# Four column pairs of an MLP's first product computed as seven block products instead of eight

## The chip, the cores and the metric

One NeuronCore of a Trainium2 chip runs the whole program in one launch. The metric is device time in microseconds (us) of that launch. PE is the tensor engine, DVE the vector engine, ACT the scalar engine, POOL GpSimd, SP the engine that issues most transfers.

## The reference

The layer has an attention part and an MLP that mixes tokens. S = 2048 tokens, D = 512 channels, F = 1792 hidden units, all in 32-bit floats.

```
h  = x + attention(layernorm(x)) @ wo            # 32 heads, linear attention
hn = layernorm(h)                                # (S, D)
u  = gelu(einsum("sd,sf->fd", hn, w1) + b1)      # (F, D): the first product
y  = einsum("fd,fs->sd", u, w2) + b2             # (S, D): the second product
out = h + y
```

The first product is a sum over the 2048 tokens for each of 1792 x 512 outputs, the second a sum over the 1792 hidden units. Each needs the matrix that the stage before it makes.

## The kernel before, in words

**Tiles.** The tokens are 16 tiles of 128 (`NT`), the hidden units 14 column blocks of 128 (`NF`), taken in 7 pairs (`NP`). PE takes its factors in a type (F32R) that holds less than a 32-bit float, so every factor is split: ACT copies it to that type (the *high* part), DVE or POOL subtracts that from the original (the *low* part), and `mm3` multiplies high by high, high by low and low by high into one accumulator. So each block product is three matmuls, at L65, L66 and L67.

**Stages.** Up to 172 us the keys and values are projected and the key-value sums are built. From 172 to 262 us the attention loop (`for it in range(NT + 4)`) runs over the token tiles: queries, `s_num`, the output projection `s_wo`, `s_h` (h = x + attention), `s_hn` (normalised h) with its split. In `s_hn` ACT writes the normalised tile to a two-buffer scratch `hn`, ACT makes its high part and POOL the low part (L61), and both are kept for all 16 tokens in tiles named `hs`. The order of PE, DVE and ACT is written out by hand in this loop (`ms`, a manual schedule), and closed behind it.

**The first product.** `fill(p)` multiplies token tile t by the two column blocks of pair p: two times three matmuls of 512 columns, with the 128x128 piece of w1 held in PE and the 512 channels of hn streamed past it. A pair is 16 such fills, 96 matmuls. `stream` brings in w1 for two token tiles at a time: one 256 KB transfer, a high copy on ACT (L614), a low subtraction on DVE (L606), each of 512 elements per partition, in rings of four buffers. Pairs 0 and 1 are filled inside the attention loop, `LAG = 5` tiles behind. The rest of pairs 0 and 1 and pairs 2 to 6 come after the loop, from 262 to 379.7 us; there a list scheduler sets the order on each engine and may move a later pair's matmul ahead of one that would wait.

**Between the products.** Behind each pair ACT applies gelu (L730). The second product is already done by seven block products, so its operands are seven 256-channel combinations of the four blocks of u: for pairs 0 and 1 made on POOL with the splits in two large pieces (`near`), for pairs 2 to 6 on DVE with 256-element splits (`far`, tiles `uf`), all of them behind the last pair.

**The second product**, from 379.7 to 518 us, takes w2 in 28 groups: a 512 KB load, three DVE sums (L785 to L787), a 1792-element high copy on ACT (L796), a 1792-element low subtraction on DVE (L805), then matmuls of 512 columns (L834) and 256 columns (L838). Its first three groups are let go by a gate, `issue_after(LO[-18])` and `issue_after(LD[-20])`, the 18th last low part and the 20th last load of w1. Its order is again by hand.

**The seven products.** With four blocks on either side of a two by two block product, the second product forms for each pair seven sums of the weight blocks and seven of the other operand, multiplies them pairwise and combines the seven results. `LAST` and `PROD` list which sum goes with which and into which accumulator.

Of the kernel before, what the change touches and what calls it, by code (L numbers as in the profile page):

```python
# [12 lines left out]
ALU = mybir.AluOpType  # L13
# [12 lines left out]
NG = 8  # L26
NPR = 2 * NG
# [9 lines left out]
def block_kernel(ctx: ExitStack, tc: tile.TileContext, x, xT, wT, phic, wo, w1, b1, w2, b2,  # L37
# [15 lines left out]
    cst.tile([P, 80], F32, name="pad")  # L53
# [15 lines left out]

    aq = ExitStack()  # L70
# [4 lines left out]
    wqh = wqp.tile([P, KD, D], F32R, name="wqh")  # L75
    wql = wqp.tile([P, KD, D], F32R, name="wql")
# [361 lines left out]
    WO = {}  # L438
    for j in range(KD):
        WO[j] = w2p.tile([P, D], F32, name=f"wo{j}")  # L440
        nc.sync.dma_start(WO[j], wo[j * P:(j + 1) * P, :])
# [76 lines left out]
    wst = ExitStack()  # L518
    wf = wst.enter_context(tc.tile_pool(name="wf", bufs=4, reuse_waits="tile"))
    a2 = ExitStack()  # L520
    ak = a2.enter_context(tc.tile_pool(name="ak", bufs=2, reuse_waits="tile"))
    ps_t = a2.enter_context(tc.tile_pool(name="ps_t", bufs=1, space=PSUM, reuse_waits="tile"))
# [52 lines left out]
    def s_h(t):  # L575

        h = HT[t]
        VE[t] = ak.tile([P, 4], F32, name="ve2", bufs=3)
        nc.vector.scalar_tensor_tensor(h, PO.pop(t), 1.0, h, op0=ALU.mult, op1=ALU.add, accum_out=VE[t][:, 2:3])
        nc.sync.dma_start(out[t * P:(t + 1) * P, :], h)  # L580

    def s_moments(t):
# [4 lines left out]
        nc.scalar.activation(VE[t][:, 0:1], VE[t][:, 3:4], AF.Identity, scale=(1.0 + EPS) / D, bias=eps2)  # L587

# [3 lines left out]
    def s_hn(t):  # L592
        nc.scalar.activation(VE[t][:, 1:2], VE[t][:, 1:2], AF.Copy, scale=r2[:, t:t + 1])
        hn = ak.tile([P, D], F32, name="hn")
# [3 lines left out]

    w1v = w1.rearrange("(k p) f -> p k f", p=P)

# [7 lines left out]
    def stream(src, k0, n, c0, w):  # L608

        raw = wf.tile([P, n, w], F32, name="wraw")  # L610
        wh_ = wf.tile([P, n, w], F32R, name="whi")
        wl_ = wf.tile([P, n, w], F32R, name="wlo")
# [34 lines left out]

    for it in range(NT + 4):
        even = it % 2 == 0
        if 0 <= it + 1 < NT:  # L650
            s_pq(it + 1)
# [7 lines left out]
        if it > 1 and even and it <= NT:  # L659
            s_num(it // 2 - 1)  # L660
        den = s_den(it + 2) if it + 2 < NT else []
# [32 lines left out]
        if not logits:  # L694
            flush()
        if 0 <= it - 2 < NT:
            s_h(it - 2)
        flush()
        for p in range(2):
# [3 lines left out]
    ms.close()  # L703
# [3 lines left out]

    up = ctx.enter_context(tc.tile_pool(name="up", bufs=1, side="right", reuse_waits="tile"))
    uo = ctx.enter_context(tc.tile_pool(name="uo", bufs=2, side="right", reuse_waits="tile"))
    ws = ctx.enter_context(tc.tile_pool(name="ws", bufs=2, side="right", reuse_waits="tile"))
# [5 lines left out]
    up.tile([P, 120], F32, name="pad")  # L724
# [7 lines left out]

    def operands_u(p):
        u = U[p]
        tt = ut.tile([P, 3, HD], F32, name="tt")
        e = nc.gpsimd if p < NEAR else nc.vector
        e.tensor_sub(tt[:, 0], u[:, 0], u[:, 1])
        e.tensor_sub(u[:, 0], u[:, 2], u[:, 0])
        e.tensor_sub(tt[:, 1], u[:, 2], tt[:, 0])
        e.tensor_sub(tt[:, 2], u[:, 3], tt[:, 1])  # L740
        if p < NEAR:
            for n0, src in ((0, u), (4, tt)):
                o = near[p][:, n0:n0 + src.shape[1]]
                split(o[:, :, 0], o[:, :, 1], src, nc.vector)
            for m in range(7):
                UB[p, m] = near[p][:, m]
            return
        for m in range(7):
            at = (p - NEAR) * 7 + m
            if at % 2 == 0:  # L750
                far[at // 2] = big.tile([P, 2, 2, HD], F32R, name="uf", tag="big")
            UB[p, m] = far[at // 2][:, at % 2]
            split(UB[p, m][:, 0], UB[p, m][:, 1], u[:, m] if m < 4 else tt[:, m - 4], nc.vector)

    for p in range(NP):
        while FN[p] < NT:
            fill(p, ps_b)
        for c in range(2):
            gelu(2 * p + c, PU[p][c])
        if p < NEAR:  # L760
            operands_u(p)
# [3 lines left out]
    hp = ctx.enter_context(tc.tile_pool(name="hp", bufs=1, reuse_waits="tile"))  # L765

# [211 lines left out]
```

## Time and profile before

| | |
|---|---|
| median of 3 runs | 523.35 us (523.15 to 523.65) |
| the profiled execution | 523.61 us |
| its span in the trace | 521.8 us |
| busy, share of the span | PE 99%, DVE 74%, ACT 54%, POOL 46% |
| granted PE clock | full in every slice of the span |

The span is what lies between the first and the last recorded instruction, 1.8 us less than the device's time. Busy shares are averages over stages with different limits. Recorded durations of neighbouring matmuls overlap: starts lie 0.22 to 0.23 us apart where durations are 0.39 us. So the pace of a row of matmuls is read from start to start, or from a stretch divided by the number of matmuls in it.

### The profile page before, as it was taken

What the parts mean: (1) busy time and instruction counts of PE and PEld (TensorE: products, weight loads), DVE (VectorE), ACT (ScalarE), POOL (GpSimd) and SP (SyncE); (2) the same over time, 40 slices, a digit from 0 to 9 for tenths busy, and PEclk for the clock granted to TensorE, in tenths of its full rate; (3) what the DMA queues carried; (4) which work ended last, traced back from release to release, by engine and by line L of the source; (5) the groups of instructions that cost most, each with busy time, mean ns of one, the idle gap of its engine ahead of it and who ended that gap; (6) DMA issues with size and microseconds to landing.
All of it is one profiled execution on the core that took longest, in us unless ns stands there. A gap on an engine that the chain in (4) does not pass through costs nothing.

```text
span 521.8 us, 8917 instructions
## 1 busy us (share of the span) xinstructions
PE 515.2 (99%) x3379; PEld 435.8 (84%) x3379; DVE 386.0 (74%) x681; ACT 282.0 (54%) x496; POOL 239.6 (46%) x188
## 2 busy tenths in 40 slices
PE   8999999999999999999999999999999999999997
PEld 7888888887877767887788888888889999999997
DVE  6893999986899998773227423725869899988985
ACT  5999853435246876666956423625553424434430
POOL 2479799985999999874425000000002112112220
PEclk9999999999999999999999999999999999999999
DMA  8644211021041324344323354532215686678734
GB/s 299 200 131 121 75 41 38 1 69 36 21 122 49 96 98 125 118 125 137 103 85 118 102 162 155 168 100 82 62 59 109 164 190 147 130 170 180 166 49 81
DMA packets 36298, 58.52 MB, mean 112 GB/s; under 512 B 3744, under 2 KB 19360, under 8 KB 36256
## 3 DMA queue, kind: packets, MB, share of 16 engines
q1 hardware_dynamic: 31936, 51.37, 31.5%
q0 software_dynamic: 4032, 6.42, 9.7%
q8 instruction: 26, 0.43, 0.4%
q10 hardware_dynamic: 288, 0.17, 0.1%
q14 instruction: 16, 0.13, 0.1%
HBM read 46.81 MB, written 11.14 MB: 111 GB/s over the span
## 4 chain that ended last, share of the span: by engine, by line
PE 89%; POOL 7%; DVE 2%; DMA 1%; issue 1%; SPq 0%; ACT 0%; POOLq 0%
PE py L834 16%; PE pu L65 12%; PE pu L66 12%; PE pu L67 11%; PE py L838 10%; PE pv L66 3%; PE pv L67 3%; PE pv L65 3%; PE pk_ps L65 2%; PE pk_ps L67 2%; PE pk_ps L66 2%; POOL ez L447 2%; POOL eq L465 2%; PE po L66 2%; PE po L65 2%; PE po L67 2%
## 5 line engine op out<-in xcount | busy, mean ns | idle before, releaser
L66 PE MATMUL pu<-hs,whi 128*128 128x512 f32 x224 | 87.7, 391 | 1.1 <-POOL hs L61 1.1
L65 PE MATMUL pu<-hs,whi 128*128 128x512 f32 x224 | 87.5, 395 | 0.0
L67 PE MATMUL pu<-hs,wlo 128*128 128x512 f32 x224 | 87.1, 390 | 0.0
L606 DVE TENSOR_TENSOR wlo<-wraw,whi 128x512 fp32r<-128x512 f32 x56 | 43.7, 784 | 53.2 <-ACT whi L614 53.0
L899 POOL DMA_DIRECT2D out<-ot x7 | 6.2, 885 | 151.1 <-DVE ot L895 151.1
L796 ACT ACTIVATE whi<-wraw 128x1792 fp32r<-128x1792 f32 x28 | 47.4, 1701 | 46.0 <-DVE wraw L787 19.8
L805 DVE TENSOR_TENSOR wlo<-wraw,whi 128x1792 fp32r<-128x1792 f32 x28 | 56.5, 2021 | 11.7 <-PE py L838 9.4
L614 ACT ACTIVATE whi<-wraw 128x512 fp32r<-128x512 f32 x56 | 34.9, 628 | 49.6 <-PE pu L66 45.3
L65 PEld LDWEIGHTS pu<-hs,whi 128*128 128x128 f32 x224 | 42.1, 188 | 10.7 <-issue 2.5
L66 PEld LDWEIGHTS pu<-hs,whi 128*128 128x128 f32 x224 | 42.1, 188 | 10.4 <-POOL hs L61 2.1
L834 PE MATMUL py<-uf,whi 128*128 128x512 f32 x175 | 49.8, 395 | 0.0
L67 PEld LDWEIGHTS pu<-hs,wlo 128*128 128x128 f32 x224 | 42.1, 188 | 8.7
L447 POOL TENSOR_TENSOR ez<-eq,zB 128x1024 f32<-128x1024 f32 x16 | 38.3, 2398 | 4.4 <-ACT zB L494 4.4
L838 PE MATMUL py<-uf,whi 128*128 128x256 f32 x210 | 39.1, 283 | 0.0
L200 POOL TENSOR_TENSOR pk<-pk,sk 128x1024 f32<-128x1024 f32 x16 | 31.0, 1940 | 7.6 <-DVE sk L199 5.1
L534 ACT ACTIVATE pht<-tn 128x512 f32<-128x512 f32 x32 | 17.4, 595 | 30.2 <-PE tn L532 30.2
L465 POOL TENSOR_TENSOR eq<-eq,w 128x1024 f32<-128x1024 f32 x16 | 32.2, 2015 | 1.3 <-DVE w L462 1.3
L838 PEld LDWEIGHTS py<-uf,whi 128*128 128x128 f32 x210 | 32.8, 192 | 0.0
L834 PEld LDWEIGHTS py<-uf,wlo 128*128 128x128 f32 x175 | 28.5, 189 | 5.0
L61 POOL TENSOR_TENSOR hs<-hn,hs 128x512 fp32r<-128x512 f32 x16 | 21.6, 1349 | 23.7 <-ACT hs L60 23.7
L204 POOL TENSOR_TENSOR zacc<-zacc,pk 128x1024 f32<-128x1024 f32 x13 | 31.3, 2405 | 0.6
L834 PEld LDWEIGHTS py<-uf,whi 128*128 128x128 f32 x175 | 29.1, 190 | 2.7
(179 smaller groups left out, 1331.9 us busy)
## 6 DMA issues: line engine op xcount, KB each, us to landing
wraw<-in_w SPq DMA_DIRECT2D x56, 256.0 KB, 2.8
wraw<-in_w SPq DMA_DIRECT2D x28, 512.0 KB, 4.4
xraw<-in_xT SPq DMA_DIRECT2D x16, 256.0 KB, 3.0
xh<-in_x SPq DMA_DIRECT2D x16, 256.0 KB, 2.7
h<-in_x SPq DMA_DIRECT2D x16, 256.0 KB, 2.7
out<-h SPq DMA_DIRECT2D x16, 256.0 KB, 2.6
out<-ot POOLq DMA_DIRECT2D x14, 256.0 KB, 4.7
wraw<-in_wT SPq DMA_DIRECT2D x12, 256.0 KB, 5.2
```

What stands on the lines that cost most here:

```text
L65: nc.tensor.matmul(o, ah, bh, start=first, stop=False)
L66: nc.tensor.matmul(o, ah, bl, start=False, stop=False)
L67: nc.tensor.matmul(o, al, bh, start=False, stop=last)
L204: nc.gpsimd.tensor_add(zacc, zacc, PK[t])
L447: nc.gpsimd.tensor_mul(EZ[t], EQ[t], zB)
L465: nc.gpsimd.tensor_mul(heads(EQ[t]), heads(EQ[t]), W[t].rearrange("p g c h -> p (g c h)").unsqueeze(2).to_broadcast([P, 2 * H, DH]))
L606: LO.append(nc.vector.tensor_sub(wl_, raw, wh_).ins)
L614: nc.scalar.activation(wh_, raw, AF.Copy)
L796: nc.scalar.activation(WH[g], RAW[g], AF.Copy)
L805: nc.vector.tensor_sub(wl_, RAW[g], WH[g])
L834: nc.tensor.matmul(o, w, u, start=p == 0 and not low, stop=p == NP - 1, skip_group_check=True)
L838: nc.tensor.matmul(bank[bk][:, half], AW[sp, p][x][:, a], UB[p, b][:, y], start=p == 0 and half == 0 and i == 0, stop=p == NP - 1 and i == ...
```

## The change

Pairs 2, 3, 4 and 5 (`SEVEN`) of the first product are computed as seven block products over pairs of token tiles. A step is one pair of columns by one pair of tokens: seven products of a 128x128 sum of w1 blocks with a 256-channel sum of normalised h blocks, three matmuls of 256 columns each, 21 in all. Eight steps make a pair and 32 the stage. Pairs 0, 1 and 6 stay as they were; pair 6 comes behind the new stage.

- **Sums of w1.** For every step DVE makes the sums in place in the raw tile (`seven_sum`: 256, 128 and 128 elements), ACT copies the 896 elements to the high part, and DVE subtracts for the low part (`seven_lo`). The rings hold 4 raw, 3 high and 3 low tiles.
- **Sums of h.** They are made once: `s_hn` now writes into a kept tile `hb`, `t_sums` forms four sums of a token pair in place, `t_hi` and `t_lo` split them (1024 elements each) into kept tiles `ht`. For token pairs 0 to 3 wholly, and for the sums of 4, this happens inside the attention loop at places given by the table `T_AT`, the rest behind it.
- **Results.** Behind each pair `seven_out` combines four accumulators on DVE (seven operations of 256) and ACT, then gelu. `near_ops` makes the operands of pairs 0 and 1 inside the new stage.
- **Order.** The manual schedule `ms` stays open to the end of the new stage. The rests of pairs 0 and 1 (`fill(0)`, `fill(1)`, `fill(1)`) stand directly behind the loop.
- **Memory.** Tiles named `hold` and `keep` are shared in turn by the query and output weights, `ht` and the w2 groups. The first w2 loads are now gated by `LO[-9]` and `LD[-8]`. The output rows of tokens 14 and 15 are sent from ACT's queue instead of SP's. The output weights `wo` are loaded into `wor`, which is free earlier, so their loads stand earlier in SP's queue.
- **Splits of `far`.** Those of pairs 2 to 6 take two sums at a time (512 elements) where they lie side by side.

```diff
@@ the attention loop @@
+    T_AT = {(13, 2): "a0 b0", (14, 1): "c0 d0", (14, 2): "a2 b2", (14, 3): "h0", (15, 0): "h1", (15, 2): "c2 d2 l0", (15, 3): "h2",
+            (16, 1): "l1", (16, 2): "l2", (17, 2): "a4 b4 c4 d4", (17, 3): "h3", (18, 2): "l3"}
...
     flush()
-    ms.close()
+    fill(0)
+    fill(1)
+    fill(1)
+    assert FN[:2] == [NT, NT]
@@ sums of normalised h @@
-        hn = ak.tile([P, D], F32, name="hn")
...
+        hn = HB[i][:, 2 * k:2 * k + 2].rearrange("p h d -> p (h d)")
...
+    def t_sums(i, half):
+
+        b = [BOTH[i // 2][:, :, m] if i < 6 else HB[i][:, m] for m in range(4)]
+        o, x, y = (((1, 0, 1), (0, 2, 0)), ((2, 2, 1), (3, 3, 2)))[half // 2][half % 2]
+        nc.vector.tensor_sub(b[o], b[x], b[y])
...
+        nc.scalar.activation(HT7[i][0], HB[i], AF.Copy)
+
+    def t_lo(i):
+        nc.vector.tensor_sub(HT7[i][1], HB[i], HT7[i][0])
@@ the new stage @@
+    AT, DEEP = {}, {"raw": 4, "hi": 3, "lo": 3}
...
+        if k == 0:
+            nc.vector.tensor_add(raw[:, 0:2], raw[:, 1].unsqueeze(1).to_broadcast([P, 2, P]), raw[:, 2:4])
+            return
+        nc.vector.tensor_add(raw[:, 4 + k], raw[:, 1 if k == 1 else 4], raw[:, 2 if k == 1 else 5])
+        if k == 2:
+            ready["hi"] += 1
+            wh_ = ring_tile("hi")
+            nc.scalar.activation(wh_, raw, AF.Copy)
...
+        for a, b, bk, half in LAST:
+            for k, (x, y) in enumerate(((0, 0), (0, 1), (1, 0))):
+                nc.tensor.matmul(ACC[p][bk][:, half], WS[p, i][x][:, a], hb[b][y],
+                                 start=i == 0 and half == 0 and k == 0, stop=i == NT // 2 - 1 and k == 2,
+                                 skip_group_check=True)
...
+    for n, (p, i) in enumerate(RUN):
+        seven_step(p, i)
+        many = 2
+        seven_lo()
+        seven_load()
+        sum_with(*todo[:many])
+        todo = todo[many:]
+        if heavy:
+            op = heavy.pop(0)
+            op and op()
+        if i == 1 and p > SEVEN[0]:
+            todo += seven_out(p - 1)
+        if i == 2 and 0 < p - SEVEN[0] <= NEAR:
+            late = near_ops(p - SEVEN[0] - 1)
...
+        if n == len(RUN) - 4:
+            fill_load(NP - 1)
+        if n >= len(RUN) - 2:
+            fill_load(NP - 1)
+            flush()
+    ms.close()
+    for op in todo + seven_out(SEVEN[-1]):
+        op()
@@ the second product @@
-    with tc.issue_after(LO[-18]), tc.issue_after(LD[-20]):
+    with tc.issue_after(LO[-9]), tc.issue_after(LD[-8]):
```

Three places show how the instructions move. The first is PE's order where the last token tile of normalised h comes in, at the end of the attention loop. In the kernel before, `hs_3168` is token tile 15, `pu_2131` an accumulator of pair 0, and `pu_3249` one of pair 2.

```order
L65 MATMUL pu_3249<-hs_2170,whi_3244 128x512
L66 MATMUL pu_3249<-hs_2170,whi_3244 128x512
L67 MATMUL pu_3249<-hs_2170,wlo_3245 128x512
L65 MATMUL pu_3250<-hs_2170,whi_3244 128x512
L66 MATMUL pu_3250<-hs_2170,whi_3244 128x512
L67 MATMUL pu_3250<-hs_2170,wlo_3245 128x512
L65 MATMUL pu_3249<-hs_2249,whi_3264 128x512
L65 MATMUL pu_2131<-hs_3168,whi_3080 128x512
L65 MATMUL pu_2132<-hs_3168,whi_3080 128x512
L65 MATMUL pu_2231<-hs_3168,whi_3125 128x512
L65 MATMUL pu_2232<-hs_3168,whi_3125 128x512
L66 MATMUL pu_3249<-hs_2249,whi_3264 128x512
```

In the kernel after, at the same place, `hs_3165` is tile 14, `hs_3190` tile 15, and `pu_2141` and `pu_2142` are the accumulators of pair 0.

```order
L66 MATMUL pu_2141<-hs_3165,whi_3097 128x512
L67 MATMUL pu_2141<-hs_3165,whi_3097 128x512
L68 MATMUL pu_2141<-hs_3165,wlo_3098 128x512
L66 MATMUL pu_2142<-hs_3165,whi_3097 128x512
L67 MATMUL pu_2142<-hs_3165,whi_3097 128x512
L68 MATMUL pu_2142<-hs_3165,wlo_3098 128x512
L66 MATMUL pu_2141<-hs_3190,whi_3097 128x512
L67 MATMUL pu_2141<-hs_3190,whi_3097 128x512
L68 MATMUL pu_2141<-hs_3190,wlo_3098 128x512
L66 MATMUL pu_2142<-hs_3190,whi_3097 128x512
L67 MATMUL pu_2142<-hs_3190,whi_3097 128x512
L68 MATMUL pu_2142<-hs_3190,wlo_3098 128x512
```

Pair 2's matmuls no longer stand between tiles 14 and 15; tile 15 of pair 0 now follows tile 14 of pair 0 at once, ahead of tile 14 of pair 1. The new stage (L903) follows tile 15 of pair 1.

The second place is DVE's order behind the last `s_h` of the loop (L579 before). Before, low parts of w1 (`wlo`) follow it one after the other.

```order
L606 TENSOR_TENSOR wlo_3081<-wraw_3079,whi_3080 128x512
L579 SCALAR_TENSOR_TENSOR h_2958,ve2_3121<-po_3096,h_2958 128x512
L606 TENSOR_TENSOR wlo_3126<-wraw_3124,whi_3125 128x512
L606 TENSOR_TENSOR wlo_3245<-wraw_3243,whi_3244 128x512
L606 TENSOR_TENSOR wlo_3265<-wraw_3263,whi_3264 128x512
L606 TENSOR_TENSOR wlo_3283<-wraw_3281,whi_3282 128x512
L606 TENSOR_TENSOR wlo_3301<-wraw_3299,whi_3300 128x512
L606 TENSOR_TENSOR wlo_3319<-wraw_3317,whi_3318 128x512
```

After, shortly behind the same `s_h`, there stand sums of w1 (L868, L870), sums of normalised h (L629), the low part of the first step (L891) and low parts of the sums of h (L641).

```order
L870 TENSOR_TENSOR wraw_3247<-wraw_3247 128x128
L629 TENSOR_TENSOR hb_3069<-hb_3069 128x256
L870 TENSOR_TENSOR wraw_3247<-wraw_3247 128x128
L868 TENSOR_TENSOR wraw_3249<-wraw_3249 128x256
L629 TENSOR_TENSOR hb_3069<-hb_3069 128x256
L870 TENSOR_TENSOR wraw_3249<-wraw_3249 128x128
L629 TENSOR_TENSOR hb_3069<-hb_3069 128x256
L870 TENSOR_TENSOR wraw_3249<-wraw_3249 128x128
L891 TENSOR_TENSOR wlo_3272<-wraw_3247,whi_3260 128x896
L641 TENSOR_TENSOR ht_3262<-hb_2762,ht_3262 128x1024
L868 TENSOR_TENSOR wraw_3251<-wraw_3251 128x256
L641 TENSOR_TENSOR ht_1737<-hb_2762,ht_1736 128x1024
```

One stream of 512-element subtractions has become a stream of 128- to 1024-element operations of four kinds.

The third place is DVE's order between the products. Before, the last `far` splits (`uf`) are followed by low parts and sums of w2 (L805, L785 to L787).

```order
L61 TENSOR_TENSOR uf_4098<-tt_4078,uf_4098 128x256
L805 TENSOR_TENSOR wlo_4175<-wraw2_4121,whi_4130 128x1792
L785 TENSOR_TENSOR wraw3_4179<-wraw3_4179 128x512
L786 TENSOR_TENSOR wraw3_4179<-wraw3_4179 128x256
L787 TENSOR_TENSOR wraw3_4179<-wraw3_4179 128x256
L805 TENSOR_TENSOR wlo_4216<-wraw0_4132,whi_4177 128x1792
L785 TENSOR_TENSOR wraw1_4220<-wraw1_4220 128x512
L786 TENSOR_TENSOR wraw1_4220<-wraw1_4220 128x256
```

After, L62 are the `far` splits, L811 to L814 their sums, L1024 the low parts of w2 and L844 to L846 its sums; `wlo1_4665` belongs to the fourth w2 group, and `u_4457` is the u of pair 6.

```order
L813 TENSOR_TENSOR tt_4530<-u_4457,tt_4530 128x256
L846 TENSOR_TENSOR wraw_4581<-wraw_4581 128x256
L1024 TENSOR_TENSOR wlo_4624<-wraw_4570,whi_4579 128x1792
L844 TENSOR_TENSOR wraw3_4628<-wraw3_4628 128x512
L814 TENSOR_TENSOR tt_4530<-u_4457,tt_4530 128x256
L62 TENSOR_TENSOR uf_4535<-u_4457,uf_4535 128x2x256
L62 TENSOR_TENSOR uf_4538<-u_4457,uf_4538 128x2x256
L62 TENSOR_TENSOR uf_4541<-tt_4530,uf_4541 128x2x256
L845 TENSOR_TENSOR wraw3_4628<-wraw3_4628 128x256
L62 TENSOR_TENSOR uf_4544<-tt_4530,uf_4544 128x256
L846 TENSOR_TENSOR wraw3_4628<-wraw3_4628 128x256
L1024 TENSOR_TENSOR wlo1_4665<-wraw_4581,whi_4626 128x1792
```

The sums and low parts of w2 now stand among the operands of the last pair instead of behind them, and the splits take up to 512 elements at a time.

230 lines of the change are left out of this document (187 added, 43 removed).

## The prediction

> **What bounds the kernel now.** I read the page first, then windows by stage, the engines' timelines around the hand-overs, and the groups of DVE and ACT.
>
> ```profile
> PE 515.2 (99%) x3379; PEld 435.8 (84%) x3379; DVE 386.0 (74%) x681; ACT 282.0 (54%) x496; POOL 239.6 (46%) x188
> PE 89%; POOL 7%; DVE 2%; DMA 1%; issue 1%; SPq 0%; ACT 0%; POOLq 0%
> ```
>
> PE is busy 515.2 of 521.8 us, and the chain that ended last runs through it for 89%. So time changes by the work taken from PE less the waits that appear on it. The windows give the stages (columns: window, length, busy and count of PE, PEld, DVE, ACT, POOL, then PE clock, DMA share, GB/s):
>
> ```profile
> 172.00:262.00 90.00, 88.85 (x598) 70.20 (x597) 61.51 (x130) 67.91 (x147) 68.49 (x51) 1.00 0.36 112
> 262.00:380.00 118.00, 118.00 (x522) 97.79 (x521) 58.58 (x105) 54.05 (x96) 9.66 (x11) 1.00 0.39 116
> 358.00:379.80 21.80, 21.80 (x98) 18.07 (x97) 15.97 (x41) 12.61 (x32) 0.00 (x0) 1.00 0.25 72
> 400.00:519.00 119.00, 118.62 (x803) 109.44 (x801) 103.83 (x156) 45.85 (x47) 23.46 (x27) 1.00 0.68 143
> ```
>
> The first product, 262 to 380 us, is bound by PE alone: no idle time in 118 us, while DVE is busy for half of it and ACT for 46%. The attention loop, 172 to 262 us, leaves PE 1.15 us of idle time and DVE 28.5. From 400 us DVE is already busy 87%, so a backlog carried over the hand-over at 380 us would be given back slowly.
>
> **PE's saving.** In the 118 us above are 522 matmuls of 512 columns: 0.226 us each (0.227 from start to start). The 256-column pace is read in the last token pair of the second product:
>
> ```profile
> 502.26 0.40 PE L838 MATMUL py<-un,whi 128*128 128x256 f32 x2
> ...
> 518.10 0.40 PE L838 MATMUL py<-uf,whi 128*128 128x256 f32 x2
> ```
>
> Between these starts lie 44 triples in 15.84 us, so 0.360 a triple and 0.120 a matmul, a little more than half of 0.227. Removed are 4 pairs x 96 = 384 matmuls: 384 x 0.227 = 87.2 us. Added are 32 steps x 21 = 672: 672 x 0.120 = 80.6 us. That is 6.5 us less, and a step lasts 2.52 us, a pair 20.2. The multiplications saved are an eighth of the pairs' columns, 10.9 of 87.2 us; the narrow form gives 4.4 of them back.
>
> [...]
>
> **DVE in the new stage.** Durations and pace, from the second product, where each operation follows another:
>
> ```profile
> 470.61 2.02 DVE L805 TENSOR_TENSOR wlo<-wraw,whi 128x1792 fp32r<-128x1792 f32 x1
> 472.54 0.68 DVE L785 TENSOR_TENSOR wraw<-wraw 128x512 f32<-128x512 f32 x1
> 473.26 0.42 DVE L786 TENSOR_TENSOR wraw<-wraw 128x256 f32<-128x256 f32 x1
> 473.72 0.42 DVE L787 TENSOR_TENSOR wraw<-wraw 128x256 f32<-128x256 f32 x1
> 474.06 2.02 DVE L805 TENSOR_TENSOR wlo<-wraw,whi 128x1792 fp32r<-128x1792 f32 x1
> ```
>
> Start to start, 1792 elements take 1.93 us, 256 before an independent operation 0.34, before a dependent one 0.46, 512 before a dependent one 0.72 (0.60 without). That is N/0.96 ns plus some 0.07 us, and 0.11 more for a dependence. So 896 elements are 1.0, 1024 are 1.13, 128 are 0.20 to 0.31. A step needs one low part and three sums: 1.0 + 0.46 + 0.31 + 0.2 = 2.0 of its 2.52 us; a pair 15.8 of 20.2. A pair also carries `seven_out` of the one before (7 x 0.34 = 2.4 at most) and, twice, near low parts (1024 and 768 elements, 2.0), so at most 20.2 of 20.2: tight. PE's cover is the ring: a low part waits only for its tile to be let go by the matmuls three steps back, so it can be ready about 3 us ahead of its use (two steps of 2.52 less its own 1.0 and the sums between). So DVE costs nothing at a steady pace; were the cover gone, each step over 2.52 us would cost its excess. If each operation cost its full duration, a step would take 1.05 + 0.42 + 2 x 0.30 = 2.07 and the 32 steps 66.2 us; with three `seven_out` of 7 x 0.42 (8.8), the near low parts (2 x 1.49 + 2 x 1.2 = 5.4) and the sums and low parts of the last two token pairs (6.4) DVE would need 86.8 us for the stage's 80.6: a rival, below. ACT copies 1792 elements in 1.70 us and 1024 in 1.07, so 896 in about 0.9: it stays over half free.
>
> ```profile
> L796 ACT ACTIVATE whi<-wraw 128x1792 fp32r<-128x1792 f32 x28 | 47.4, 1701 | 46.0 <-DVE wraw L787 19.8
> L60 ACT ACTIVATE un<-u 128x1024 fp32r<-128x1024 f32 x2 | 2.1, 1066 | 0.0
> L61 DVE TENSOR_TENSOR un<-u,un 128x1024 fp32r<-128x1024 f32 x2 | 3.0, 1490 | 0.5 <-ACT un L60 0.5
> ```
>
> POOL collides with DVE:
>
> ```profile
> 256.99 0.69 DVE L606 TENSOR_TENSOR wlo<-wraw,whi 128x512 fp32r<-128x512 f32 x1
> 262.43 1.09 DVE L606 TENSOR_TENSOR wlo<-wraw,whi 128x512 fp32r<-128x512 f32 x1
> 261.68 1.30 POOL L61 TENSOR_TENSOR hs<-hn,hs 128x512 fp32r<-128x512 f32 x1 [1.92 <-ACT hs L60]
> 275.94 0.73 POOL L739 TENSOR_TENSOR tt<-u,tt 128x256 f32<-128x256 f32 x1
> 276.75 1.07 POOL L740 TENSOR_TENSOR tt<-u,tt 128x256 f32<-128x256 f32 x1
> ```
>
> The same subtraction takes 1.09 instead of 0.69 us beside a POOL operation that ends at 262.98. [...] `near_ops` puts eight such POOL subtractions (0.73 to 1.07 us) into two pairs: up to 3 us more DVE time in each, out of a lead of 3 us. I take nothing for it, up to 2 us at the bad end.
>
> **In the loop.** Sums and low parts of h go into DVE's idle time before `s_h`:
>
> ```profile
> 256.37 0.69 DVE L579 SCALAR_TENSOR_TENSOR h<-po,h 128x512 f32<-128x512 f32 x1 [2.02 <-POOL r L590]
> 261.81 0.69 DVE L579 SCALAR_TENSOR_TENSOR h<-po,h 128x512 f32<-128x512 f32 x1 [4.14 <-issue]
> ```
>
> Two or four 512-element operations (1.2 to 2.7 us) and low parts (1.13) fit gaps of 2.0 and 4.1 us. The tight place is `h2` (ACT, 1.07 us), which stands before the last attention `oh`:
>
> ```profile
> 251.37 1.06 ACT L557 ACTIVATE oh<-tn 128x512 fp32r<-128x512 f32 x2
> 252.47 1.29 DVE L562 TENSOR_TENSOR ol<-tn,oh 128x512 fp32r<-128x512 f32 x2 [2.08 <-ACT oh L557]
> 253.85 0.39 PE L67 MATMUL po<-woh,ol 128*128 128x512 f32 x1
> ```
>
> The first of the two `ol` ends at about 253.1, PE wants it at 253.85: 0.75 us of cover for 1.07, so 0 to 0.5 us is paid; I take 0.3. The moved `wo` loads stand earlier on SP's queue, ahead of an input tile of the first stage; DMA is the releaser on 1% of the chain, so I take 0, up to 0.5. The output rows sent from ACT instead of SP cost ACT an issue each, and SP's loads behind them no longer wait for `s_h`; ACT is idle before 271 us anyway.
>
> **The start of the stage.** Before, pair 2's matmuls stood between token tiles 14 and 15. Now tile 15 comes at once. The first matmul behind the attention's last is at 261.56; 24 matmuls stand ahead of tile 15, so PE wants it at 261.56 + 24 x 0.227 = 267.0:
>
> ```profile
> 261.56 0.39 PE L65 MATMUL pu<-hs,whi 128*128 128x512 f32 x1
> 266.34 0.62 ACT L60 ACTIVATE hs<-hn 128x512 fp32r<-128x512 f32 x1
> 267.04 1.29 POOL L61 TENSOR_TENSOR hs<-hn,hs 128x512 fp32r<-128x512 f32 x1 [2.48 <-ACT hs L60]
> 271.70 1.28 ACT L730 ACT_TABLE_LOAD   x1
> 274.42 1.26 ACT L730 ACTIVATE u<-pu,b1s 128x512 f32<-128x512 f32 x2
> ```
>
> Its high part is ready at 266.96, its low part at 268.33, one matmul after 267.23: a wait of 0.6 to 1.2 us, taken as 0.9. At about 271.7 the stage starts. Its first high parts share ACT with other work. From 266.96 ACT has three high parts of 896 (0.9) and three of 1024 (1.0) in turn, the table load (1.28), four gelus (4 x 0.58 start to start) and then the fourth high part: 266.96 + 5.7 + 1.28 + 2.3 + 0.9 = 277.1, some 278.2 with the gaps between. DVE's low part follows 1.1 later, at 279.3. PE's fourth step begins at 271.7 + 3 x 2.52 = 279.3 and wants it two matmuls on. It comes 0 to 1 us late, the latter if a POOL subtraction of `near_ops` stands in DVE's way; I take 0.5.
>
> **The hand-over.** After the stage's end E, PE has 21.8 us of pair 6 and then the second product. Pair 6 needs low parts of 512, and its second shares a ring tile with its first, so it waits for the matmuls of the first to end: by the paces 0.4 us, and 0.1 at the third; 0.5 in all, between 0 and 1. DVE's order from the last `seven_out` to the low part of the fourth w2 group (`wlo1_4665`) holds 39 operations of 256, 20 of 512 and 4 of 1792: 39 x 0.34 + 20 x 0.60 + 4 x 1.93 = 33.0 us, with dependences about 34.5. Before, DVE had only 15.97 us to do in the 21.80 at that place. Part of the list behind the second product's gate now stands among pair 6's own low parts in DVE's queue, so a w2 load that lands late would hold up pair 6. Counting PE's order from E at 0.227 and 0.120, PE wants this low part at about E + 33.7, and with the waits above at 34.2. The wait is 0 to 2 us (2 if DVE has to wait for ACT on the way); I take 1.0, since no list of this length runs without a gap. The second group's low part is ready at about E + 24, wanted at 26.9. Wider `far` splits (512 in 0.60 for twice 0.34) save DVE time alone.
>
> **The sum.** -6.5 + 0.3 (loop) + 0.9 + 0.5 (start) + 0.5 (pair 6) + 1.0 (hand-over) = -3.3 us. The profiled execution took 523.61 us, 0.26 above the median of 523.35. It becomes 520.3, the median 520.0. A measurement of this kernel can tell about 0.2%, 1.05 us, from no change.
>
> **The rivals.**
>
> *All covers hold (0.14).* Ring leads make up the waits: 523.35 - 6.5 = 516.9. For it: DVE and ACT are half idle there now; against it: tile 15's wait, which nothing covers.
>
> *DVE paces the stage (0.12), the slower side.* Its place is the rings of `wg`. It decides from the point at which a step's DVE work, averaged over a pair, is over 2.52 us. Full durations give 86.8 us against 80.6: the saving is gone, and with the terms at start and hand-over the time is 523.35 - 6.5 + 6.2 + 2.9 = about 526; 525 with a lead kept. For it: those 20.2 us in the two pairs with near operations, and near low parts whose mean was 1.49 beside POOL. Against it: operations in a row start closer than their durations, and two pairs have slack of 2 us.
>
> *The backlog at the hand-over is larger (0.14).* DVE is 87% busy after 400 us, so anything late there is paid by PE. If ACT and DVE wait for each other in the new interleaving of w2 sums, operands and splits, each 1792-element low part comes 1 to 2 us later than its matmuls: three groups, 3 to 6 us more than I took: 523 to 526. For it: my 33.0 us lets DVE wait for nothing. Against it: 20 us of pair 6 in which late work can still be caught up.
>
> *The weight loads set the spacing (0.03).* If a matmul of 256 columns cannot start before its own weight load has run its length, the narrow form saves nothing. In the last window above loads are busy 109.44 us for 801: 0.137 each. 672 x 0.137 = 92.1 us against 87.2, and with the waits 523.35 + 4.9 + 3.2 = 531. Against it: the 44 triples at 0.120 had a load for every matmul too. [...]
>
> **How the numbers follow.** The forecast has 0.57. All waits at their lower ends (0, 0.6, 0, 0.5, 0) give 518.0, at their upper ends (0.5, 1.2, 1, 0.5, 2, and 2 of collisions) 524.0; as they will not all fall together its own range is 518.3 to 522.2. Below it lies 0.14 at about 517. Above lie 0.29, of which I take in those up to 525. Range 516.6 to 525.0. Faster by over 0.2% (under 522.3): 0.57 + 0.14 + 0.01 = 0.72. Within 0.2% (522.3 to 524.4): the better half of the hand-over rival and a little of the DVE rival, 0.10. Slower: 0.18.
>
> **What would show it.** Right: from the last attention matmul on, PE idles in a few places of under 1.5 us (behind tile 14, once in the first four steps, in pair 6 and in the first three w2 groups); 256-column matmuls in the stage start 0.12 us apart, and a pair takes 20.2 us. Wrong: PE waits every step for `wlo` L891 with DVE near 100% (DVE paces); PE waits over 3 us for L1024 or `uf` after pair 6 (backlog); steps over 2.6 us without waits (weight loads).

## The result, and the profile after

| | before | after |
|---|---|---|
| median of 9 runs | 523.15 us (522.74 to 523.65) | 525.48 us (523.85 to 527.03) |
| ratio | 1 | 1.0048 (95%: 1.0036 to 1.0059) |
| the profiled execution, and its span | 523.61, 521.8 | 527.01, 525.2 |

The kernel became 2.3 us slower where 3.3 us less were forecast. The profiled execution is one of four in which PE's mean granted clock was 0.997 (525.8 to 527.0 us); the five with 1.0 took 523.9 to 525.5.

First the busy line of the page after, then windows of the changed kernel over the stretch that the change touches (columns as before the change).

```profile
PE 515.2 (98%) x3667; PEld 445.2 (85%) x3667; DVE 457.8 (87%) x820; ACT 299.3 (57%) x495; POOL 247.6 (47%) x188
```

```profile
262.00:269.00 7.00, 7.00 (x32) 5.66 (x31) 6.86 (x11) 5.71 (x13) 4.42 (x4) 1.00 0.20 74
269.00:278.00 9.00, 7.45 (x27) 5.45 (x26) 8.26 (x18) 7.01 (x10) 1.29 (x1) 0.81 0.21 61
278.00:300.00 22.00, 22.00 (x187) 22.00 (x186) 20.62 (x39) 12.17 (x14) 5.76 (x4) 1.00 0.35 98
300.00:340.00 40.00, 39.70 (x332) 39.50 (x332) 38.17 (x79) 21.32 (x26) 4.67 (x4) 1.00 0.37 103
340.00:380.00 40.00, 39.67 (x253) 35.99 (x253) 37.93 (x82) 24.32 (x38) 0.00 (x0) 1.00 0.43 134
262.00:400.00 138.00, 134.86 (x936) 125.37 (x935) 130.98 (x259) 80.23 (x114) 16.35 (x14) 0.99 0.36 109
```

The same last window of the kernel before:

```profile
262.00:400.00 138.00, 138.00 (x651) 116.00 (x650) 75.01 (x135) 63.63 (x111) 10.70 (x12) 1.00 0.37 108
```

PE's total busy time is the same 515.2 us although 6.5 us of matmuls were taken away. DVE went from 75 to 131 of these 138 us: what was a stage with half of DVE free has become one in which DVE is busy 95%. In the second window the granted clock is 0.81.

The timeline of PE in the changed kernel, from the last attention matmul to the end of the slow stretch (before, the same last matmul stood at 261.33):

```profile
263.95 0.39 PE L68 MATMUL po<-woh,ol 128*128 128x512 f32 x1
...
268.63 0.40 PE L67 MATMUL pu<-hs,whi 128*128 128x512 f32 x1
...
269.57 0.40 PE L68 MATMUL pu<-hs,wlo 128*128 128x512 f32 x1
270.64 0.50 PE L66 MATMUL pu<-hs,whi 128*128 128x512 f32 x1 [0.68 <-ACT hs L61]
272.01 0.50 PE L67 MATMUL pu<-hs,whi 128*128 128x512 f32 x1 [0.87 <-POOL hs L62]
...
272.83 0.63 PE L67 MATMUL pu<-hs,whi 128*128 128x512 f32 x1
273.26 0.63 PE L68 MATMUL pu<-hs,wlo 128*128 128x512 f32 x1
...
275.82 0.58 PE L68 MATMUL pu<-hs,wlo 128*128 128x512 f32 x1
276.23 0.40 PE L66 MATMUL pu<-hs,whi 128*128 128x512 f32 x1
```

Three things are to be seen. The attention ends 2.6 us late, before any matmul of the new stage. From 268.63 to 269.57 four matmuls take 0.235 us each, not 0.227. Tile 15's high and low parts are waited for (2.1 us lost from start to start), and behind that PE runs at half speed from 272.83 to 276.23, eight matmuls 0.427 apart at a granted clock of 0.50.

By stage, span against span (521.84 and 525.23 us):

| place | forecast | measured | read from |
|---|---|---|---|
| matmuls of the four pairs | -6.5 | -6.5 | an undisturbed pair takes 20.1 us (297.70 to 317.78) |
| up to the last attention matmul | +0.3 | +2.6 | 263.95 against 261.33 |
| from there through the first seven-product pair | +1.4 | +3.9 | 33.75 us; PE needs 0.23 + 42 x 0.227 + 20.16 = 29.9 |
| the other three pairs | 0 | +0.4 | 297.70 to 359.48, 61.8 less 0.93 of pair 6 (below), for 60.5 |
| pair 6 and the rest | +1.5 | +2.9 | 165.75 from 359.48 on and those 0.93; 163.76 before |
| sum | -3.3 | +3.3 | spans differ by 3.4 |

Four matmuls of pair 6 stand inside the last step of the stage, ahead of its low part, so their 0.93 us are counted with pair 6:

```profile
356.28 0.40 PE L66 MATMUL pu<-hs,whi 128*128 128x512 f32 x1
...
356.98 0.40 PE L67 MATMUL pu<-hs,whi 128*128 128x512 f32 x1
357.21 0.28 PE L903 MATMUL pu<-hs,wlo 128*128 128x256 f32 x1
```

Of the 3.9 us, 2.1 are tile 15's two waits, 1.6 the eight matmuls at half speed (0.2 us too long each) and 0.2 the slower fills.

### The profile page after: what moved, and what is told of

It reads as the page before. It is cut to its first block, busy times and chain, and to the rows that moved or that the text cites. A ratio compares the mean times of both kernels' runs of the same rounds, so it can differ in the third digit from the quotient of the medians.

```text
span 525.2 us, 9658 instructions
## 1 busy us (share of the span) xinstructions
PE 515.2 (98%) x3667; PEld 445.2 (85%) x3667; DVE 457.8 (87%) x820; ACT 299.3 (57%) x495; POOL 247.6 (47%) x188
## 5 line engine op out<-in xcount | busy, mean ns | idle before, releaser
L1024 DVE TENSOR_TENSOR wlo<-wraw,whi 128x1792 fp32r<-128x1792 f32 x28 | 56.5, 2020 | 6.1 <-PE py L1056 5.3
L874 ACT ACTIVATE whi<-wraw 128x896 fp32r<-128x896 f32 x32 | 30.5, 952 | 38.6 <-DVE wraw L870 26.0
L903 PE MATMUL pu<-ht,whi 128*128 128x256 f32 x256 | 47.2, 282 | 0.0
L67 PE MATMUL pu<-hs,whi 128*128 128x512 f32 x96 | 38.9, 405 | 2.0 <-POOL hs L62 2.0
L66 PE MATMUL pu<-hs,whi 128*128 128x512 f32 x96 | 39.6, 413 | 0.7 <-ACT hs L61 0.7
L903 PEld LDWEIGHTS pu<-ht,whi 128*128 128x128 f32 x256 | 39.7, 191 | 0.0
L68 PE MATMUL pu<-hs,wlo 128*128 128x512 f32 x96 | 37.7, 401 | 0.3 <-DVE wlo L659 0.3
L903 PE MATMUL pu<-ht,wlo 128*128 128x256 f32 x128 | 36.1, 282 | 0.0
L891 DVE TENSOR_TENSOR wlo<-wraw,whi 128x896 fp32r<-128x896 f32 x32 | 34.9, 1092 | 1.3 <-ACT whi L874 1.3
L903 PE MATMUL pu<-hs,whi 128*128 128x256 f32 x192 | 35.9, 283 | 0.0
L62 POOL TENSOR_TENSOR hs<-hb,hs 128x512 fp32r<-128x512 f32 x16 | 22.2, 1385 | 22.8 <-ACT hs L61 20.8
L1056 PEld LDWEIGHTS py<-uf,whi 128*128 128x128 f32 x210 | 32.7, 192 | 0.0
```

What stands on the lines that cost most here:

```text
L66: nc.tensor.matmul(o, ah, bh, start=first, stop=False)
L67: nc.tensor.matmul(o, ah, bl, start=False, stop=False)
L68: nc.tensor.matmul(o, al, bh, start=False, stop=last)
L891: nc.vector.tensor_sub(wl_, raw, wh_)
L903: nc.tensor.matmul(ACC[p][bk][:, half], WS[p, i][x][:, a], hb[b][y], start=i == 0 and half == 0 and k == 0, stop=i == NT // 2 - 1 and k == ...
L1024: nc.vector.tensor_sub(wl_, RAW[g], WH[g])
```

## The experiments

Each was timed beside the kernel before on the same chip. Distances between operands are worked out from the addresses of the tiles in the built programs of these runs, and every pace is read from their traces; the traces do not hold addresses, so what the runs show is how the pace moves when an edit shifts one side or both.

**Where tiles begin.** The first 2.6 us lie where no matmul was added. One line that the excerpt of the diff left out shortens a pad:

```diff
-    cst.tile([P, 80], F32, name="pad")
+    cst.tile([P, 64], F32, name="pad")
```

Every tile of the left side (xs, hs, oh and others) begins 64 bytes lower, and the right side's wqh 32 bytes off. The first experiment is this edit alone, made in the kernel before.

> The kernel before with its first pad tile 64 bytes shorter, so that every tile of the left side of on-chip memory (xs, hs, wvh, the w1 rings, oh, ol) begins 64 bytes lower, as in the changed kernel; nothing else. Theory 1, where an operand begins sets PE's pace, each operand for itself: 512-column matmuls in the first 262 us at about 230 ns instead of 227 and the last attention matmul 2 to 3 us later; the fills of 262 to 380 us at 230 too, so some 1.5 to 2 us more there; 526 to 528 us. Theory 2, only the distance between the two operands counts: projections with weights of the right side (wkh, wqh) slower, fills (hs and whi both moved) unchanged at 227; about 524.5. Theory 3, the layout is not it, the slow pace is a state of that execution: 227 everywhere and 523.2.

523.31 against 522.91 us, 1.0007 (0.9997 to 1.0016). The time hides two opposite moves. The last attention matmul of this kernel:

```profile
262.80 0.39 PE L67 MATMUL po<-woh,ol 128*128 128x512 f32 x1
```

That is 1.5 us later than the 261.33 before, projections running at 230 ns; the second product, 136.4 us from its first to its last matmul instead of 138.5, gives 2.1 back. The fills behind the loop, whose operands moved together, keep 227 ns, all but the first ten, which stand behind slower matmuls and start 231.7 ns apart in the mean. The short rows of fills inside the loop (231 ns) and the first ten of most rows of `wvh` projections, whose operands moved together too, show the same. Theory 1 fails on the fills, theory 3 on the projections; 2 stands, but about ten matmuls behind a slow row were slow too (231.7 ns).

```diff
+    cst.tile([P, 64], F32, name="pad")      # left side
+    wqp.tile([P, 520], F32, name="pad")     # right side, 504 before
```

> The kernel before with left and right side tiles of its first two stages both 64 bytes lower, so that all distances between the operands of a matmul stay as they were while each begins 64 bytes off. Theory 1 (each operand for itself): slower than with the left side alone, 527 to 529 us, projections at 230 ns or more. Theory 2 (distance): 523.2 and 227 ns. Theory 3 (a state of the execution): 523.2.

521.36 us, 0.9966 (0.9953 to 0.9979), faster than any theory said. Projections and fills are back at 227 ns, so in these runs the pace went with the distance, as theory 2 has it. The gain is the second product, where weights had not moved and streamed tiles had: 231.3 ns instead of 232.6 at 512 columns, 116.0 instead of 119.1 at 256.

```diff
-    ones ... r2 = cst.tile(...)
+    ones ... r2 = top.tile(...)             # a pool at the upper end
...                                          # its pad and that of cst
-    wqp.tile([P, 504], F32, name="pad")
+    wqp.tile([P, 512], F32, name="pad")
-        junk = ak.tile([P, D], F32, name="hj", bufs=1)
+        junk = ak.tile([P, D + 104], F32, name="hj", bufs=1)[:, :D]
```

> The changed kernel with the same instructions in the same order, but its constants moved to the upper end of memory and three pads changed, so that all tiles that PE reads begin at multiples of 512 bytes again. Theories 1 and 2: 512-column matmuls before 262 us at 227 ns, the last attention matmul at about 261.5 us instead of 263.95, the whole 2 to 3 us faster, 522.5 to 523.5; the wait for token tile 15 and the slow clock behind it stay. Theory 3: 525.5 and the last attention matmul at 264 as often as before.

523.35 us, 1.0007 (0.9994 to 1.002): 2.1 us below the changed kernel, as theories 1 and 2 said. This is the realigned kernel of what follows. The last attention matmul:

```profile
260.80 0.39 PE L70 MATMUL po<-woh,ol 128*128 128x512 f32 x1
```

The stretch from here through the first pair is still 33.4 us (to 294.16). So the layout accounts for the first term of the error, and not for the second.

**The start of the stage.** In the changed kernel, tile 14 of pair 1 is put ahead and h3, l3 later.

```diff
-    fill(0)
     fill(1)
+    fill(0)
     fill(1)
-(17, 3): "h3", (18, 2): "l3"}
+(18, 2): "h3", (19, 2): "l3"}
```

> The changed kernel with two moves: tile 14 of pair 1 stands ahead of tile 15 of pair 0 on PE, and the high and low parts of the fourth sum of h (h3, l3) come one turn of the loop later, so that they no longer stand on ACT ahead of the normalised h of tile 14. Theory: the two waits behind tile 14 (1.02 and 1.14 us of lost time in the profile) shrink to under 0.7 in sum and the granted clock stays 1.0 behind them, so that 1.4 us of waits and, in the executions that had it, 1.7 us of half-speed matmuls go: 523 to 523.8 instead of 525.5. Rival: the wait is set by the chain through ACT and POOL further ahead (tile 15's own attention), so PE still waits over 1.5 us and the clock falls in some executions: 525.

527.06 us, 1.0077 (1.0062 to 1.0092). Neither theory's time holds. The wait for tile 15 is gone (0.3 us left) and the clock stays 1.0, but PE now waits for three low parts and a high part of w1 in the first five steps, the longest here:

```profile
279.18 0.39 PE L903 MATMUL pu<-hs,wlo 128*128 128x256 f32 x1 [1.42 <-DVE wlo L891]
```

The stretch grew to 35.0 us. Tile 15's wait had been hiding a backlog on DVE, to which this edit adds l3. The next two test that on the realigned kernel.

```diff
     def t_four(i):
-        return [lambda k=k: t_sums(i, k) for k in range(4)]
+        return [None] * 4
     def t_lo(i):
+        if i > 3:
+            nc.gpsimd.memset(HT7[i][1].bitcast(F32), 0.0)
+            return
```

> The realigned changed kernel without eight sums of normalised h (token pairs 6 and 7) and four of their low parts (pairs 4 to 7, filled with zeros on POOL instead), some 8 us less DVE work around the start of the new stage; the output differs by that. Theory A, DVE paces the start: in the realigned kernel PE needs 29.9 us for the matmuls from the end of the attention to the end of the first seven-product pair and takes 33.4, with DVE busy throughout; without the 8 us the stretch falls to 30 to 31 us and the time by 2.5 to 3.5, to about 520.5. Theory B, token tile 15's chain through ACT and POOL sets the start and DVE is only busy beside it: the stretch stays over 32.5 us, 522.5 to 523.4.

The lighter kernel: 522.26 us, 0.9992 (0.9974 to 1.0011); the stretch 32.3 us (260.41 to 292.75), between the two. The wait for DVE that the realigned kernel had in the fifth step (0.83 us from start to start, ending at 284.15) is gone. Tile 15's two waits (0.98 and 0.86 us idle) are not, and they are the 2.4 us by which the stretch still exceeds PE's 29.9. So of the 3.5 us that the realigned kernel loses there, DVE's work is 1.0 and tile 15's chain 2.4. The clock blurs the median: the five executions with a mean clock of 1.0 have 521.55, the five with 0.995 to 0.997 have 523.8 (realigned: 522.7 in four, 523.7 in six).

```diff
-SEVEN = (2, 3, 4, 5)
+SEVEN = (3, 4, 5)
+    for k in range(NT // 2):
+        ...
+        fill(2, ps_b)
+        fill(2, ps_b)
+        ...                       # three of the operations on h
```

> The realigned changed kernel with three pairs of seven products (3, 4, 5) and pair 2 plain, placed ahead of them; the sums of h, their high and low parts and the first sums of w1 are spread beside its 21.8 us of matmuls. Theory A (DVE paces the start): the 3.5 us lost there go but for tile 15's own wait of about 1, one pair's saving of 1.6 us is given up, so about 522.5, and each seven-product pair takes 20.2 us. Theory B (tile 15's chain): the loss at the start stays and 1.6 us are given up, 525.

526.01 us, 1.0063 (1.004 to 1.0086), above both theories. At the start theory A holds but for tile 15's wait: the first seven-product pair begins at 294.6, 2.2 us after PE's own 292.4, nearly all of it tile 15's waits, and takes 20.1. But the loss comes back at the hand-over. A window there and PE's longest wait:

```profile
380.00:396.00 16.00, 13.36 (x81) 11.52 (x80) 15.93 (x29) 8.39 (x12) 0.00 (x0) 1.00 0.42 132
```

```profile
394.18 0.50 PE L1064 MATMUL py<-uf,whi 128*128 128x512 f32 x1 [2.40 <-DVE uf L64]
```

DVE is busy 15.93 of 16 us: the work taken from the start is not gone. Next, which chain makes tile 15 late:

```diff
-(17, 2): "a4 b4 c4 d4", (17, 3): "h3", (18, 2): "l3"}
+(19, 2): "a4 b4 c4 d4 h3 l3"}
```

> The realigned changed kernel with the four sums of token pair 4 and h3, l3 moved behind the last normalised h in the loop, the order of the fills as in the change. Theory: these stood on ACT ahead of tile 14's normalised h and beside POOL's small power operations, and so delayed tile 15; its two waits shrink from 2.3 us to 1.0 to 1.5, near the 0.6 to 1.2 of the prediction, but the moved DVE work then delays the first steps by as much, so 523 to 524.5 in all. Rival: tile 15's chain is late for another reason, waits of 2 us or more and the rest unchanged.

526.9 us, 1.0077 (1.0055 to 1.0099). The waits for tile 15 fell less than expected, from 1.86 us of idle time in the realigned kernel (2.4 lost from start to start) to 1.40 (1.9):

```profile
267.12 0.50 PE L68 MATMUL pu<-hs,whi 128*128 128x512 f32 x1 [0.56 <-ACT hs L63]
268.47 0.50 PE L69 MATMUL pu<-hs,whi 128*128 128x512 f32 x1 [0.84 <-POOL hs L64]
```

From tile 15's `s_h` on DVE to the end of its power on POOL (`r`, which scales the normalised h) it is 2.7 us before the change, 4.3 in the realigned kernel and still 4.0 here. The four sums now run beside POOL's low part of tile 14 and that power:

```profile
262.44 3.83 DVE L631 TENSOR_TENSOR hb<-hb 128x512 f32<-128x512 f32 x4
```

```profile
262.55 1.72 POOL L64 TENSOR_TENSOR hs<-hb,hs 128x512 fp32r<-128x512 f32 x1 [1.94 <-ACT hs L63]
264.23 1.00 POOL L607 TENSOR_TENSOR r<-ve,mhalf 128x1 f32<-128x1 f32 x1
```

The moved work delayed the first steps by more than expected; the stretch is 36.9 us. Last, both limits at once, with the edits of the kernel with the other order and of the lighter one together:

> The realigned changed kernel with both moves at the start: the lighter DVE work (sums of token pairs 6 and 7 and low parts of 4 to 7 left out, zeros instead; the output differs by that), and tile 14 of pair 1 ahead of tile 15 with h3 and l3 one turn later. Theory: the start has two limits, DVE's work and tile 15's chain, and each run so far took away one and ran into the other; with both gone the stretch from the last attention matmul to the end of the first seven-product pair falls from 33.4 to 30 to 30.7 us, and the time to 519.5 to 520.5. Rival: a third wait (ACT's chain of high parts) takes their place: over 31.5 us, 521.5 or more.

521.81 us, 0.9976 (0.9965 to 0.9988), and the stretch is 32.0 us: the rival is right, there is a third limit. Tile 15 is waited for 0.37 us, the fourth step 1.02. PE, and ACT ahead of it:

```profile
280.59 0.39 PE L908 MATMUL pu<-hs,wlo 128*128 128x256 f32 x1 [1.02 <-DVE wlo L896]
```

```profile
274.45 1.28 ACT L792 ACT_TABLE_LOAD   x1
275.75 2.42 ACT L792 ACTIVATE u<-pu,b1s 128x512 f32<-128x512 f32 x4
278.05 1.80 ACT L879 ACTIVATE whi<-wraw 128x896 fp32r<-128x896 f32 x2
```

DVE was idle 2.97 us ahead of that low part, for the high part at 278.05 behind the table load and the gelus. It is the chain that the prediction named for the fourth step.

**Can POOL help DVE?** In the realigned kernel every other low part of w1 goes to POOL:

```diff
-        nc.vector.tensor_sub(wl_, raw, wh_)
+        (nc.gpsimd if ready["lo"] > 4 and ready["lo"] % 2 else nc.vector).tensor_sub(wl_, raw, wh_)
```

> The realigned changed kernel with every other low part of the new stage's w1 blocks on POOL instead of DVE, 14 of 32. DVE gives up 14 x 1.0 us. If two engines can subtract side by side, DVE's waits in the stage go and the time falls 1 to 2 us. If a DVE operation waits while a POOL operation reads memory (as the long low parts beside POOL suggest), a POOL subtraction of about 2.2 us holds DVE up for longer than the 1.0 us it saves, and the stage gets slower: 525 to 529. I expect the latter.

533.75 us, 1.0206 (1.019 to 1.0222), slower still than expected. DVE and POOL at one such place:

```profile
309.35 1.88 DVE L872 TENSOR_TENSOR wraw<-wraw 128x128 f32<-128x128 f32 x1
```

```profile
308.96 2.12 POOL L893 TENSOR_TENSOR wlo<-wraw,whi 128x896 fp32r<-128x896 f32 x1 [3.29 <-ACT whi L876]
```

A sum of 128 elements that takes 0.28 us elsewhere lasts 1.88 and ends 0.15 us after POOL's subtraction at 311.08. At the next such place two of them take 2.51 us from 316.47, where two in a row take 0.60 elsewhere, and end 0.14 us after POOL's subtraction (2.13 us from 316.71). In this kernel idle POOL time was no room for DVE's work of this kind.

**The 64 bytes used on purpose.** Rings of both products 64 bytes further, in the realigned kernel:

```diff
+    wst.enter_context(tc.tile_pool(name="gap", bufs=1, reuse_waits="tile")).tile([P, 16], F32, name="pad")
...
-        WH[g] = keep([P, 7, GRP * P], F32R, "whi", g % 3)
+        WH[g] = off(keep([P, OFF + 7 * GRP * P], F32R, "whi", g % 3))
```

> The realigned changed kernel with the weight rings of the new stage and of the second product 64 bytes further (the identity and the mask moved into another pool to make room), so that weight and streamed operand of the narrow matmuls begin 64 bytes apart modulo 512. With both shifted alike or not at all the narrow form took 119 to 120 ns, with streamed tiles 64 bytes below the weights 113 to 115 in the second product of the kernel with both sides lowered. Theory: distance sets the pace, so the new stage's 672 matmuls take 113.5 to 115 (3.5 to 4.4 us less) and the second product's 2 to 3 us less; DVE then paces two of the pairs, so 517 to 519. Rival: the narrow pace there came from something else, and it stays at 523.4.

521.75 us, 0.9961 (0.9944 to 0.9979), short of the theory's 517 to 519. Two triples of this kernel's stage, then two of the changed kernel's:

```profile
306.02 0.39 PE L906 MATMUL pu<-ht,whi 128*128 128x256 f32 x2
306.25 0.28 PE L906 MATMUL pu<-ht,wlo 128*128 128x256 f32 x1
306.36 0.39 PE L906 MATMUL pu<-ht,whi 128*128 128x256 f32 x2
```

```profile
309.86 0.40 PE L903 MATMUL pu<-hs,whi 128*128 128x256 f32 x2
310.10 0.28 PE L903 MATMUL pu<-hs,wlo 128*128 128x256 f32 x1
310.22 0.40 PE L903 MATMUL pu<-hs,whi 128*128 128x256 f32 x2
```

0.34 us a triple instead of 0.36. Over the whole stage the mean is 115.4 ns instead of 120, so 3.1 us of matmuls went in the stage alone, but 1.6 us of the median in all: where PE is quicker it waits more for DVE (0.77, 0.53 and 0.59 us idle at 284, 318 and 332 in the stage, 0.67 and 0.22 in the realigned kernel, and 1.50 for DVE's output step at 451).

This edit and the one with three pairs together:

> Three pairs of seven products behind plain pair 2, with the 64-byte distance as well. If both theories hold the gains add but for DVE's limit in two pairs: 522.5 less 5 to 6 us, 516.5 to 518. If only the distance matters 519; if neither 525.

525.84 us, 1.0048 (1.0031 to 1.0065), no faster than without the distance. Narrow matmuls at 113.9 ns, and the same waits at the hand-over: DVE sets that end.

```diff
+    ws.tile([P, 16], F32, name="pad", bufs=1)   # behind the second product's rings
```

> The kernel before with one more 64-byte pad behind the second product's rings, so that its weights begin 64 bytes below the streamed operands modulo 512; the order of the instructions is the same. If the distance sets the narrow pace, its 588 matmuls of 256 columns fall from 119.1 to about 115 ns and the time by 2 to 3 us, to 520 to 521, faster than the kernel before and the changed one. Rival: only streamed operands below the weights help, not above: 523.

520.56 us, 0.9953 (0.994 to 0.9965), as the theory said: faster than the kernel before and the changed one, with 64 bytes of pad and no change of work. Its 588 narrow matmuls take 116.1 ns instead of 119.1, its wide ones in a row 228.9 instead of 232.6.

## Why the prediction was wrong

**PE's saving** was right: 20.1 us a pair, 120 ns a matmul. **The hand-over** was right in kind and nearly in size. PE's two waits there:

```profile
359.96 0.72 PE L68 MATMUL pu<-hs,wlo 128*128 128x512 f32 x2 [0.33 <-DVE wlo L659]
...
395.03 0.39 PE L1052 MATMUL py<-uf,wlo 128*128 128x256 f32 x1 [0.97 <-DVE wlo L1024]
```

The end of the stage is 359.48. The second wait, for the fourth group's low part, was forecast at 34.2 us behind it with 1.0 us, and came at 34.4 with 1.13 from start to start; the first was forecast with 0.4 and cost 0.5. The other 1.4 us of the +2.9 are a wait for DVE's output step that ends at 454.65 and was not foreseen. DVE waits there for ACT, and ACT for an output transfer that POOL issued at 448.20 and that took 5.4 us to land:

```profile
453.69 0.94 ACT L1105 ACTIVATE low<-py 128x256 f32<-128x256 f32 x3 [4.93 <-DMA out<-low]
```

A wait of 1.50 us stands there in one other trace (the kernel with 64 bytes on purpose), none in the realigned kernel; why the transfer lands late in some stays open.

**"In the loop"** was sized 0.3 and measured 2.6. The wait for `ol` is 0.2 of that, near the forecast. The rest is the pace of matmuls that the change does not touch, from 20 us on; the prediction read an instruction diff and took the pace of unchanged matmuls as given. The realigned kernel took that term back (2.1 us in the medians).

**"The start of the stage"** was sized 1.4 (0.9 for tile 15, 0.5 for step four) and measured 3.9. The step that failed is the wait for tile 15: 2.1 us, and 1.6 more at half speed behind it, which the sum did not have. In step four, and anywhere else in the first pair, the trace shows no wait of PE. The prediction took the time at which tile 15 is ready from the kernel before, and asked only when PE would want it. But the new work stands in the way of tile 15's chain, which is 4.3 us instead of 2.7 from `s_h` to the end of the power: ACT comes to it 1.2 us later, since `h3` and tile 14's normalised h stand ahead, and powers on POOL last longer beside DVE's sums and low parts of h. ACT, DVE and POOL, in the changed kernel (the three powers are those of tiles 13, 14 and 15):

```profile
263.21 1.07 ACT L638 ACTIVATE ht<-hb 128x1024 fp32r<-128x1024 f32 x1
```

```profile
257.26 2.33 DVE L641 TENSOR_TENSOR ht<-hb,ht 128x1024 fp32r<-128x1024 f32 x1
...
260.72 3.84 DVE L629 TENSOR_TENSOR hb<-hb 128x512 f32<-128x512 f32 x4
```

```profile
258.46 1.53 POOL L605 TENSOR_TENSOR r<-ve,mhalf 128x1 f32<-128x1 f32 x1
...
263.24 0.99 POOL L605 TENSOR_TENSOR r<-ve,mhalf 128x1 f32<-128x1 f32 x1
...
268.03 0.73 POOL L605 TENSOR_TENSOR r<-ve,mhalf 128x1 f32<-128x1 f32 x1
```

Before, the same power on POOL:

```profile
255.47 0.55 POOL L590 TENSOR_TENSOR r<-ve,mhalf 128x1 f32<-128x1 f32 x1
```

The collision was in the prediction's rows, but only as time that DVE loses. The 2 us for collisions at the upper end of its range, an estimate, did not come: beside the POOL subtractions of `near_ops` from 318.49 to 323.32 us PE does not wait, and its only wait in the stage from 278 us on is 0.30 us, at 336.03.

A second limit lies behind the first. DVE's work was summed for a steady pair (20.2 of 20.2) and said to fit, but not for the stretch that comes first, where sums of token pairs 4, 6 and 7, four low parts of h and the sums that fill the rings are added. From 262 to 300 us DVE is busy 35.7 of 38 us (the windows above). In the changed kernel tile 15's wait covers this; with that wait gone (the other order) PE waits for DVE and ACT instead, and in the realigned kernel DVE's work costs 1.0 us beside tile 15's 2.4. No run shows a start that is free of all three limits, tile 15, DVE and ACT.

Most signs that the prediction gave for being right are there (a few waits under 1.5 us, 0.12 us a matmul, 20.1 us a pair), and the median is 5.5 us above its 520.0: none of them looked at the pace of unchanged matmuls, or at the clock.

**The rivals.** "DVE paces the stage" had 0.12. At its price, 6 us from the sum of full durations over four pairs, it did not come: the last three pairs lost 0.4 us. What it names is a limit at the start, and wherever PE is made quicker. "The backlog at the hand-over" did not come in this kernel, but did in the one with three pairs. The weight-load rival is out: 120 ns and less in every trace.

**The half-speed stretch** adds its own length: the four executions of the changed kernel with a mean clock of 0.997 are 1.6 us longer in the median than the five with 1.0 (526.7 and 525.1), and eight matmuls at 0.2 us more are 1.6.

**What stays open:** why the pace moves with the distance of the operands (227 and 230 ns in the kernel with the left side lowered), why about ten matmuls behind a slow row were slow too (231.7 ns there), and why one distance had two paces: in the kernel with 64 bytes on purpose most steps of the stage run at 113.3 ns, others at 117.8.

## What to carry to other kernels

When work is taken from the bound engine by giving sums to another, add up that other engine's work for every stretch, the filling of the rings above all, and not only for a steady step, and follow the chain of the last operand through every engine that got new work: here tile 15 came late through ACT and POOL, in a stretch that PE could have done 3.9 us sooner. Compare where the operands of matmuls begin before and after a change of memory pools: here unchanged matmuls became 1 to 4% slower or faster (227 ns to 230 and 233, 120.0 to 115.4). An engine that looks idle may be no help: here a POOL subtraction of 2.12 us went with a DVE sum of 1.88 us instead of 0.28, and the kernel took 533.75 us instead of 523.35.

## What the runs showed of the hardware

- **Distance of operands.** Mean spacing of matmuls in a row, read from the traces of these runs, by the distance (less whole multiples of 512 bytes, from the addresses in their programs) between the starts of the streamed operand and the weights:

| distance | 512 columns | 256 columns |
|---|---|---|
| 0 | 227 ns (fills and projections, kernel before) | 120.0 (stage, realigned) |
| 64 bytes | 230 (wkh, wqh projections, left side lowered) | 115.4 (stage, 64 bytes on purpose; 113.3 or 117.8 in a step) |
| 32 or 96 bytes (fills in the loop, wqh; changed kernel) | 233 | 118.0 (sums of h of token pairs 0 to 2, distance 32) |

  In the second product, where both forms alternate, both were faster with the distance (232.6 to 231.3 and 119.1 to 116.0 in the kernel with both sides lowered).
- **The clock.** In the profiled execution of the changed kernel two waits that cost 2.1 us, within 2.8 us, were followed by 3.4 us at half speed: PE was busy 1.86 of the 3.41 us from 269.39 to 272.80 at a granted clock of 1.00, and from 272.83 to 276.23 the clock was 0.50. In that of the realigned kernel the same two waits cost 2.4 us, and the clock was 1.00 all the way from 262 to 300 us. In that of the kernel with low parts on POOL it was 1.00 from 300 to 340 us, with PE busy 34.52 of 40 us, and 0.96 from 340 to 380, with PE busy 36.77. So a short wait may or may not be followed by half speed, and what decides was not shown. The mean clock was under 0.999 in four of nine executions of the changed kernel, six of ten of the realigned and five of ten of the lighter one, and in none of the 14 of the two kernels with the other order.
- **DVE and POOL.** Operations beside each other took longer on both: POOL's power 1.53 us beside a low part of h on DVE (changed kernel; 0.55 before), DVE's sum of 128 elements 1.88 us beside a low part of w1 on POOL (2.12 us; 0.28 elsewhere).
